# Last stage of a three-stage kernel: first blocks loaded during the d_ff stage into their own place, later loads ordered behind each unit's blocks, output product in order

## The chip, the cores and the metric

The kernel runs on one core of a Trainium2 chip. The metric is the device time of one execution in microseconds. TensorE (PE) does the matmuls and its weight loads (PEld), VectorE (DVE), ScalarE (ACT) and GpSimd (POOL) the elementwise work; loads and stores are issued from the queue of SyncE (SP), a few from POOL's.

## The reference

Three stages follow each other on 4608 tokens (8 batches of 576). Attention over a memory of 32 slots for each head gives x with 512 features; a layer with d_ff = 2048 and the activation h - tanh(h) gives x again; the last stage is a maximum over three projections and an output product:

```python
h = x @ w_in                       # 512 -> 2048
g = h - np.tanh(h)
x = g @ w_out                      # 2048 -> 512
h = np.maximum(np.maximum(x @ w1, x @ w2), x @ w3)   # 512 -> 768 each
return h @ w_out                   # 768 -> 512
```

## The kernel before

Everything is float32. A product that must keep its precision is made of three matmuls on operands split in a high part (rounded to float32r) and a low part (the rest): high x high, high x low, low x high. Splitting an operand costs a ScalarE copy (the high part) and a subtraction on VectorE or POOL (the low part).

The attention and d_ff stages run together up to about 821 us. `steps` lists the d_ff work: a tile of tokens and one of 16 chunks of 128 features; `emit_h` makes h, `emit_g` the activation, `emit_x` adds the chunk's contribution to four PSUM banks. At a tile's last chunk, VectorE adds the banks to `xo` and SP stores it in `xd[1]` (L531). Smaller work of other stages is dealt out in `slot()` as background; there `Paced` (L48) orders an instruction of VectorE, ScalarE or PE behind that engine's `mark`, the last instruction of the main work, without a semaphore.

The last stage works on six groups of 768 tokens. Each group has nine units (three column blocks `jp` by three projections `w`). A unit multiplies a block `sw` of weights with the group's x in the seven-product scheme of Strassen and Winograd: operands B11, T3, T1, B21, T2, B22, T4 (L633), seven products of six matmuls each with 384 columns, 42 in all, in four of six rotating PSUM banks. Between them ScalarE copies (p1, p5, u2), and VectorE and POOL add into `c` and take the running maximum in `m`. After the third projection of a column block, `m` is split into `mh` (L788 to L794), the upper half `q` 0 and 1 and one quarter on POOL, one quarter on VectorE. After nine units `outs` makes the output product: for each of six blocks of 128 tokens, 18 matmuls of 512 columns (six rows `j` of the weights `wz`), with banks b0 and b1 in turn, a copy into `ob`, and four stores.

The weights `sw` were laid out in DRAM as nine blocks of 1792 KB, and each unit loads its own again: four buffers sw0 to sw3, and `load_sw(n + 4)` at the end of unit n (L784), so that a load waits for the unit that used its buffer. `xprep` (L649) and `split` (L636) prepare a group's operands: the first group's during d_ff (`first_x`, a hook sixteen steps before the end of d_ff, L682; T4's split after it, L734), a later group's inside `outs` from `xr`, four parts of 384 KB loaded at the group's unit 0 (L839).

All memory of the last stage besides B11 to B22 (mv0 to mv5) comes from the pool `l`, which lies on the memory of attention and d_ff; a tile waits for the last reader of what lay there. The first four blocks are loaded after d_ff's instructions, three of them from POOL's queue (L733), the fourth and the six parts of `wz` from SP (L736 to L739). A program orders each engine's instructions ahead of time by when it expects them to be ready; on the chip each engine and each queue goes through its list in order. SP's transfers use eight semaphores in turn, so that a transfer's issue also waits for the eighth before it to land.

Of the kernel before, what the change touches and what calls it, by code (L numbers as in the profile page):

```python
# [7 lines left out]
F32 = mybir.dt.float32  # L8
F32R = mybir.dt.float32r
# [13 lines left out]
def kernel(  # L23
# [24 lines left out]
    class Paced:  # L48
# [4 lines left out]
        def __getattr__(self, name):  # L53
            op = getattr(self.engine, name)

            def call(*a, **kw):
                i = op(*a, **kw)  # L57
                if self.mark is not None and background[0]:
                    tc.add_manual_dep(i.ins, self.mark.name, mybir.DependencyInfo(mybir.DependencyClass.NoSync, mybir.DependencyReason.DATA), reason="pace")
                return i  # L60

            return call

    background = [False]
    V, S, T = (Paced(e) for e in (nc.vector, nc.scalar, nc.tensor))
    G, DMA = nc.gpsimd, nc.sync
    B, H, NS, D = q.shape
    M = phi.shape[3]
    P = 128
# [39 lines left out]
    def f(x):  # L109
        return x.bitcast(F32)  # L110
# [523 lines left out]
    mv_p, mv = [], {}  # L634

    def split(i, y, eng):  # L636
        t = get("mv6") if i == T4 else mv_p[0].tile([P, 2, 2, NQ], F32R, tag=f"mv{i}", bufs=1, name=f"mv{i}")
        S.copy(t[:, 0], y)
        yield
        if eng is G:  # L640
            for c in range(2):
                G.tensor_sub(t[:, 1, c], y[:, c], f(t[:, 0, c]))  # L642
                yield
        else:
            eng.tensor_sub(t[:, 1], y, f(t[:, 0]))
            yield
        mv[i] = t

    def xprep(x):  # L649
        b11, b12, b21, b22 = x  # L650
        yield from split(B11, b11, V)
        V.tensor_sub(b11, b12, b11)
        yield
        V.tensor_sub(b12, b22, b12)
        yield
        yield from split(T3, b12, G)
        yield from split(T1, b11, V)
        yield from split(B21, b21, G)
        V.tensor_sub(b11, b22, b11)
        yield  # L660
        yield from split(T2, b11, V)
        yield from split(B22, b22, G)
        V.tensor_sub(b21, b21, b11)
        yield

    def x_load(x, g):
        for y, kc, h in zip(x, (0, 0, 2, 2), (0, 1, 0, 1)):
            DMA.dma_start(out=y, in_=xd[1][:, kc:kc + 2, g * NG + h * NQ:g * NG + (h + 1) * NQ])

    def first_x():  # L670
        while bg.q:
            bg.step(10 ** 9)
        prep_s.close()
        pre_p = pool("pre", stack=last, side="right")
        mv_p.append(pre_p)
        x = [(pre_p if t == "xe" else cv_p).tile([P, 1024], F32, tag=t, bufs=n, name="xq")[:, :2 * NQ].rearrange("p (k c) -> p k c", k=2)
             for t, n in (("raw", 2), ("raw", 2), ("xe", 1), ("cs", 1))]
        x_load(x, 0)
        first_x.x = x
        bg.add("x", xprep(x), start[2, 0] - 12)  # L680
# [1 line left out]
    hooks[start[2, 0] - 16] = [first_x]  # L682
    run(start[1, 0], start[2, 0])
    wo1_p.__exit__(None, None, None)
    main.close()


    last2 = ExitStack()
    l_p = pool("l", stack=last2)
    ps_b = pool("ps_b", PSUM, last2)  # L690

    fresh = {}

    def lay(tag, shape, dt=F32, p=l_p):
# [7 lines left out]
    lay("sw0", [P, 2, 14, P], F32R)  # L702
    lay("mv6", [P, 2, 2, NQ], F32R)
    for i in range(3):
        lay(f"mh{i}", [P, 2, 2, NG], F32R)
    for n in ("p1", "p5", "u2"):
        for i in range(2):
            lay(f"{n}{i}", [P, NQ])
    for i in range(2):
        lay(f"ob{i}", [P, DM])  # L710
    lay("c", [P, 4, NQ])
    lay("gap", [P, 512])
    for i in (1, 2):
        lay(f"sw{i}", [P, 2, 14, P], F32R)
    for i in range(2):
        lay(f"m{i}", [P, 4, NQ])
    lay("wz", [P, J, 2, DM], F32R)
    lay("xr", [P, 4, 2, NQ])
    lay("sw3", [P, 2, 14, P], F32R)
    for i in range(8):  # L720
        lay(f"b{i}", [P, 512], F32, ps_b)

    sw_t = {}
    NU = 9 * GR

    def load_sw(n, dma=DMA):
        if n < NU:
            t = sw_t[n] = get(f"sw{n % 4}")
            dma.dma_start(out=f(t), in_=sw_d[n % 9])

    bg.need("x")
    for n in range(3):
        load_sw(n, G)  # L733
    for _ in split(T4, first_x.x[2], V):  # L734
        pass
    load_sw(3)  # L736
    wz = get("wz")
    for j in range(J):
        DMA.dma_start(out=f(wz[:, j]), in_=wz_d[j])  # L739

    free = [6, 7, 4, 5, 2, 3]
    acc, mh_t = [None], {}
# [1 line left out]
    def unit(n):  # L744
        jp, w = divmod(n % 9, 3)
        sw = sw_t.pop(n)
        ids = [free.pop(0) for _ in range(4)]
        A, Bk, Ck, Dk = (get(f"b{i}")[:, :NQ] for i in ids)
        i = n % 2

        def prod(o, s, x, first, final):
            for kc in range(2):
                st = sw[:, :, 2 * s + kc]
                x0, x1 = mv[x][:, 0, kc], mv[x][:, 1, kc]
                for k, (lt, rt) in enumerate(((st[:, 0], x0), (st[:, 0], x1), (st[:, 1], x0))):
                    T.matmul(o, lt, rt, start=first and kc == 0 and k == 0, stop=final and kc == 1 and k == 2, skip_group_check=True)

        if w == 0:
            acc[0] = get(f"m{jp % 2}")
        m = acc[0]  # L760

        c = m if w == 0 else get("c")

        def upd(q):
            if w:
                V.tensor_max(m[:, q:q + 2], c[:, q:q + 2], m[:, q:q + 2])

# [12 lines left out]
        prod(Ck, 6, B22, False, True)  # L780
        V.tensor_add(c[:, 1], Ck, u2)
        upd(0)
        prod(Bk, 2, T4, False, True)
        load_sw(n + 4)  # L784
        V.tensor_add(c[:, 2], Bk, u2)
        upd(2)
        free.extend(ids[k] for k in (3, 0, 2, 1))
        if w == 2:  # L788
            mh = mh_t[jp] = get(f"mh{jp}")
            for q, nq, e in ((0, 2, G), (3, 1, G), (2, 1, V)):  # L790
                h, t = divmod(q, 2)
                y, o = m[:, q:q + nq].rearrange("p a c -> p (a c)"), slice(t * NQ, (t + nq) * NQ)
                S.copy(mh[:, 0, h, o], y)
                e.tensor_sub(mh[:, 1, h, o], y, f(mh[:, 0, h, o]))  # L794

    def outs(g):
        ps = {}

        def part(u, js):
            if u not in ps:  # L800
                ps[u] = get(f"b{u % 2}")
            o = slice(u * P, (u + 1) * P)
            for j in js:
                mh = mh_t[j // 2][:, :, j % 2, o]
                mm3(ps[u], (mh[:, 0], mh[:, 1]), (wz[:, j, 0], wz[:, j, 1]), j == 0, j == J - 1)

        def done(u):
            ob = get(f"ob{u % 2}")
            (S.copy if u % 2 else V.tensor_copy)(ob, ps[u])
            for r in range(0, P, 32):  # L810
                b, j = divmod((g * NG + u * P + r) // 32, TJ)
                dst = out[b * NS:(b + 1) * NS, :].rearrange("(p j) e -> j p e", j=TJ)
                DMA.dma_start(out=dst[j], in_=ob[r:r + 32, :])

        prep = iter(())
        if g + 1 < GR:
            x = [xr[:, k] for k in range(4)]
            prep = chain(xprep(x), split(T4, x[2], V))
        for u in range(6):
            if u == 0:  # L820
                part(0, range(4))
                part(1, range(4))
                part(0, range(4, J))
            elif u == 1:
                part(1, range(4, J))
            else:
                part(u, range(J))
            done(u)
            for _ in range(6):
                next(prep, None)  # L830
# [42 lines left out]
```

## Time and profile before

| | us |
|---|---|
| median of 3 runs | 1394.51 (1391.09 to 1396.32) |
| the profiled execution | 1389.84 |
| its span, first to last instruction | 1388.1 |
| TensorE busy | 1289.5 (93%) |
| VectorE busy | 741.0 (53%) |
| POOL busy | 586.6 (42%) |
| ScalarE busy | 507.2 (37%) |

The profiled execution's time is its span and 1.7 us around it. Busy times are sums over the whole program; what a stage is bound by is read from the timeline, the windows and the waits of that stage. A matmul's record is longer than the time until the next one starts, because matmuls overlap: the pace is read from a run of many.

### The profile page before, as it was taken

The numbers are of one execution on the slowest core, as the hardware profiler recorded it, in microseconds if no ns is written. First come the engines' busy times: TensorE is split into PE (matmuls) and PEld (weight loads), VectorE is DVE, ScalarE is ACT, GpSimd is POOL, SyncE is SP. The second block draws the span as 40 slices with busy tenths as digits, with TensorE's granted clock in tenths as the row PEclk, the third lists the DMA queues.
The fourth block names the chain that finished last, engine by engine and source line by source line (L and its number), as shares of the span: only waits on it lengthen the run. The fifth ranks groups of instructions, "written<-read, shape, count | busy, mean of one in ns | idle before, by whom it ended". The sixth has DMA issues, their size and how long they took to land.

```text
span 1388.1 us, 22726 instructions
## 1 busy us (share of the span) xinstructions
PE 1289.5 (93%) x8996; PEld 1156.9 (83%) x8996; DVE 741.0 (53%) x1147; ACT 507.2 (37%) x993; POOL 586.6 (42%) x505
## 2 busy tenths in 40 slices
PE   3568888999999999999999989999999999999998
PEld 1446776887887798898889989989999899899996
DVE  4758646676445655765643333635734646357342
ACT  2425334454343554555544322322312223123121
POOL 4446334563323546675764332422512424235121
PEclk9979999999999999999999999999999999999999
DMA  8774747767524536666573159556656656565531
GB/s 222 175 205 150 177 146 203 179 210 187 137 102 171 176 117 233 228 210 253 206 252 117 50 217 411 213 197 237 233 168 250 235 175 218 192 247 190 166 134 46
DMA packets 179690, 264.94 MB, mean 191 GB/s; under 512 B 85760, under 2 KB 151552, under 8 KB 170496
## 3 DMA queue, kind: packets, MB, share of 16 engines
q1 hardware_dynamic: 178384, 256.80, 56.7%
q0 software_dynamic: 1200, 6.69, 1.4%
q8 instruction: 71, 1.16, 0.4%
q14 instruction: 35, 0.29, 0.1%
HBM read 199.49 MB, written 63.96 MB: 190 GB/s over the span
## 4 chain that ended last, share of the span: by engine, by line
PE 71%; DMA 10%; DVE 7%; POOL 6%; SPq 2%; ACT 2%; issue 2%; ACTq 0%; DVEq 0%; POOLq 0%
PE b L57 32%; PE ps_x L57 23%; PE ps_h L57 12%; DMA sw<-sw_d 3%; POOL mv L642 2%; PE ps_kv L57 2%; DVE cvb L57 2%; PE ps_w L57 2%; DMA wz<-wz_d 1%; SPq L198 1%; DMA raw<-in_moe_w_in_dram 1%; DMA kv<-in_v_dram 1%; POOL mh L794 1%; DVE s L57 1%; DVE st L57 1%
## 5 line engine op out<-in xcount | busy, mean ns | idle before, releaser
L57 PE MATMUL ps_x<-gh,wo 128*128 128x320 f32 (+2 forms) x2400 | 451.7, 335 | 14.9 <-DVE xo L57 10.4
L57 PEld LDWEIGHTS ps_x<-gh,wo 128*128 128x128 f32 x2400 | 379.6, 190 | 64.2 <-issue 22.9
L57 PE MATMUL b<-mv,sw 128*128 128x384 f32 x2268 | 410.3, 340 | 5.0 <-DMA sw<-sw_d 5.0
L57 PEld LDWEIGHTS b<-mv,sw 128*128 128x128 f32 x2268 | 403.7, 189 | 9.1 <-DMA sw<-sw_d 4.0
L496 POOL TENSOR_TENSOR gh<-th,gh 128x320 fp32r<-128x320 f32 (+2 forms) x200 | 210.4, 1054 | 241.2 <-ACT gh L57 232.4
L57 PE MATMUL ps_h<-at,vw 128*128 128x256 f32 (+2 forms) x1536 | 251.1, 304 | 29.2 <-ACT at L57 14.3
L57 PEld LDWEIGHTS ps_h<-at,vw 128*128 128x128 f32 x1536 | 225.2, 194 | 55.4 <-ACT at L57 16.1
L57 DVE TENSOR_TENSOR th<-ps_h,th 128x320 f32<-128x320 f32 (+2 forms) x200 | 106.7, 537 | 184.1 <-ACT th L57 182.5
L57 ACT ACTIVATE th<-ps_h 128x320 f32<-128x320 f32 (+2 forms) x200 | 94.9, 478 | 179.0 <-PE ps_h L57 173.1
L57 PE MATMUL b<-wz,mh 128*128 128x512 f32 x648 | 157.5, 393 | 2.9 <-POOL mh L794 2.3
L779 POOL TENSOR_TENSOR c<-c,u 128x384 f32<-128x384 f32 x36 | 40.1, 1113 | 276.0 <-ACT u L57 276.0
L57 PEld LDWEIGHTS b<-wz,mh 128*128 128x128 f32 x648 | 120.3, 188 | 29.6 <-POOL mh L794 4.3
L57 ACT CAST gh<-th 128x320 fp32r<-128x320 f32 (+2 forms) x200 | 99.7, 499 | 98.1 <-DVE th L57 84.8
L57 ACT COPY p<-b 128x384 f32<-128x384 f32 x108 | 51.8, 479 | 165.6 <-PE b L57 165.6
L794 POOL TENSOR_TENSOR mh<-m,mh 128x768 fp32r<-128x768 f32 (+1 forms) x36 | 67.8, 1903 | 50.8 <-ACT mh L57 50.8
L57 DVE TENSOR_TENSOR c<-b,u 128x384 f32<-128x384 f32 x72 | 39.7, 552 | 87.8 <-PE b L57 87.8
L57 DVE TENSOR_SCALAR cvb<-cvb 128x512 f32<-128x512 f32 x112 | 66.3, 592 | 32.6 <-ACT cvb L57 30.6
L57 DVE TENSOR_TENSOR m<-c,m 128x768 f32<-128x768 f32 x72 | 73.7, 1024 | 4.1
L57 DVE TENSOR_TENSOR vw<-ps_w,vw 128x512 fp32r<-128x512 f32 x64 | 41.4, 682 | 35.5 <-ACT vw L57 35.5
L57 DVE TENSOR_TENSOR c<-b,p 128x384 f32<-128x384 f32 x72 | 37.6, 554 | 42.1 <-ACT p L57 40.5
L642 POOL TENSOR_TENSOR mv<-xr,mv 128x384 fp32r<-128x384 f32 x30 | 45.0, 1524 | 28.7 <-ACT mv L57 28.7
L57 DVE COPY ob<-b 128x512 f32<-128x512 f32 x18 | 12.4, 689 | 81.3 <-PE b L57 81.3
(82 smaller groups left out, 1069.3 us busy)
## 6 DMA issues: line engine op xcount, KB each, us to landing
sw<-sw_d SPq DMA_DIRECT2D x51, 1792.0 KB, 7.4
sw_d<-so SPq DMA_DIRECT2D x9, 1792.0 KB, 6.2
raw<-in_moe_w_out_dram SPq DMA_DIRECT2D x22, 512.0 KB, 4.1
at_d<-at SPq DMA_DIRECT2D x16, 576.0 KB, 3.8
at<-at_d SPq DMA_DIRECT2D x8, 1152.0 KB, 6.2
raw<-in_moe_w_dram SPq DMA_DIRECT2D x18, 512.0 KB, 4.9
out_dram<-ob SPq DMA_DIRECT2D x144, 64.0 KB, 1.7
xd<-xo SPq DMA_DIRECT2D x14, 640.0 KB, 4.7
```

The source lines that it names most:

```text
L57: i = op(*a, **kw)
L198: q_dma.dma_start(out=t[64 * e + 32 * h:64 * e + 32 * h + 32, r], in_=src[e, h, r])
L496: G.tensor_sub(gh[:, 1], th, f(gh[:, 0]))
L642: G.tensor_sub(t[:, 1, c], y[:, c], f(t[:, 0, c]))
L779: G.tensor_add(c[:, 3], c[:, 3], u2)
L794: e.tensor_sub(mh[:, 1, h, o], y, f(mh[:, 0, h, o]))
```

## The change

The first block (sw0) gets a place in the pool `pre` beside mv0 to mv3, and `first_x` loads it on SP in front of the first group's x. x itself lies in an `at` buffer and in `cs`. A new pool `r`, opened after the last d_ff step on the place of d_ff's second-half output weights, holds mv4 to mv6, `xr`, `c` and the two `ob`; the splits of T2, B22 and T4 (`xrest`) come there, after the last d_ff step. Blocks 1 and 2 are still loaded from POOL's queue, block 3 from SP. The parts of `wz` are loaded one at a time at units 2 to 7 of the first group, and `xr` at unit 8 in the first group and unit 2 in the others, each ordered on SP behind the last block load. In `outs`, the matmuls are ordered behind the last unit's matmuls (`T.mark`), and the preparation of the next group behind the mh instructions of its engine (`S.mark`, `e.mark`), for which POOL is `Paced` too. The first half of `mh` (q 0 and 1) goes from POOL to VectorE. Its core:

```diff
-    V, S, T = (Paced(e) for e in (nc.vector, nc.scalar, nc.tensor))
-    G, DMA = nc.gpsimd, nc.sync
+    V, S, T, G = (Paced(e) for e in (nc.vector, nc.scalar, nc.tensor, nc.gpsimd))
+    DMA = nc.sync
...
-        yield from split(T2, b11, V)
-        yield from split(B22, b22, G)
         V.tensor_sub(b21, b21, b11)
         yield
...
+    def xrest(x):
+        return chain(split(T2, x[0], V), split(B22, x[3], G), split(T4, x[2], V))
...
+        sw_t[0] = pre_p.tile([P, 2, 14, P], F32R, tag="sw0", bufs=1, name="sw0")
+        DMA.dma_start(out=f(sw_t[0]), in_=sw_d[0])
+        t = at_p.tile([P, 3, 2, NQ], F32, tag="at", bufs=3, name="xq")
+        u = cv_p.tile([P, 1024], F32, tag="cs", bufs=1, name="xq")[:, :2 * NQ].rearrange("p (k c) -> p k c", k=2)
+        x = [t[:, 0], t[:, 1], u, t[:, 2]]
         x_load(x, 0)
...
+    r_p = pool("r", stack=last, side="right")
...
+    for _ in xrest(first_x.x):
+        pass
+    main.close()
...
-    for n in range(3):
+    for n in (1, 2):
         load_sw(n, G)
-    for _ in split(T4, first_x.x[2], V):
-        pass
     load_sw(3)
     wz = get("wz")
-    for j in range(J):
-        DMA.dma_start(out=f(wz[:, j]), in_=wz_d[j])
...
-                    T.matmul(o, lt, rt, start=first and kc == 0 and k == 0, stop=final and kc == 1 and k == 2, skip_group_check=True)
+                    T.mark = T.matmul(o, lt, rt, start=first and kc == 0 and k == 0, stop=final and kc == 1 and k == 2, skip_group_check=True).ins
...
-            for q, nq, e in ((0, 2, G), (3, 1, G), (2, 1, V)):
+            for q, nq, e in ((0, 2, V), (3, 1, G), (2, 1, V)):
...
-                S.copy(mh[:, 0, h, o], y)
-                e.tensor_sub(mh[:, 1, h, o], y, f(mh[:, 0, h, o]))
+                S.mark = S.copy(mh[:, 0, h, o], y).ins
+                e.mark = e.tensor_sub(mh[:, 1, h, o], y, f(mh[:, 0, h, o])).ins
...
         def part(u, js):
+            background[0] = True
...
+            background[0] = False
...
+            background[0] = True
             for _ in range(6):
                 next(prep, None)
+            background[0] = False
...
-            if n == 0 and g + 1 < GR:
+            late = []
+            if g == 0 and 2 <= n < 2 + J:
+                late.append(DMA.dma_start(out=f(wz[:, n - 2]), in_=wz_d[n - 2]))
+            if n == (2 if g else 8) and g + 1 < GR:
                 xr = get("xr")
-                x_load([xr[:, k] for k in range(4)], g + 1)
+                late += x_load([xr[:, k] for k in range(4)], g + 1)
+            for d in late:
+                behind(d.ins, load_sw.last)
```

`behind` is the ordering without a semaphore that `Paced` used before, as a function. `load_sw` now keeps its last load in `load_sw.last`.

## Rows read from the trace of the kernel before

**Rows 1.** The page, part 1: busy us (share of the span), instructions.
```profile
PE 1289.5 (93%) x8996; PEld 1156.9 (83%) x8996; DVE 741.0 (53%) x1147; ACT 507.2 (37%) x993; POOL 586.6 (42%) x505
```

**Rows 2.** Timeline of PE: start, length, tile, count, idle before and releaser.
```profile
814.08 6.76 PE L57 MATMUL ps_x<-gh,wo 128*128 128x320 f32 x45
824.56 30.44 PE L57 MATMUL b<-mv,sw 128*128 128x384 f32 x156 [3.72 <-DMA sw<-sw_d]
856.30 15.92 PE L57 MATMUL b<-mv,sw 128*128 128x384 f32 x89 [1.30 <-DMA sw<-sw_d]
```

**Rows 3.** Windows: length, each engine's busy time (count), granted clock, DMA share, GB/s.
```profile
730.00:760.00 30.00, 30.00 (x230) 26.99 (x229) 12.17 (x24) 13.44 (x29) 12.20 (x13) 1.00 0.37 127
...
820.80:824.50 3.70, 0.04 (x1) 0.00 (x0) 1.75 (x4) 0.00 (x0) 0.00 (x0) 0.88 0.98 415
824.50:832.00 7.50, 7.44 (x27) 7.44 (x28) 0.80 (x2) 0.96 (x2) 0.00 (x0) 0.60 1.02 417
...
840.00:848.00 8.00, 8.00 (x48) 8.00 (x47) 4.00 (x6) 1.44 (x3) 1.02 (x1) 1.00 1.03 402
...
883.30:907.30 24.00, 23.62 (x127) 22.23 (x126) 19.78 (x21) 10.16 (x17) 14.26 (x10) 1.00 0.62 229
```

**Rows 4.** Chain in order of time, 815 to 910: start, length, what.
```profile
823.97 19.39 DMA wz<-wz_d
...
843.43 12.73 DMA sw<-sw_d
```

**Rows 5.** Waits of PE, 860 us to the end: total, times, longest.
```profile
PE b L57 <- POOL mh L794: 2.3, 6, 0.4
```

**Rows 6.** Timeline, last group: two runs of matmuls without a break.
```profile
1339.72 15.70 PE L57 MATMUL b<-mv,sw 128*128 128x384 f32 x88
...
1366.61 16.66 PE L57 MATMUL b<-wz,mh 128*128 128x512 f32 x72 [0.56 <-DVE ob L57]
```

**Rows 7.** Timeline of SP near 735 us: the first load of x.
```profile
734.74 0.37 SPq L668 DMA_DIRECT2D xq<-xd  x1
```

**Rows 8.** Timeline around the end of d_ff: splits, block loads, last sums.
```profile
795.35 2.00 POOL L642 TENSOR_TENSOR mv<-xq,mv 128x384 fp32r<-128x384 f32 x2 [0.21 <-ACT mv L57]
...
804.57 3.29 POOL L642 TENSOR_TENSOR mv<-xq,mv 128x384 fp32r<-128x384 f32 x2 [1.80 <-ACT mv L57]
...
815.70 0.83 ACT L57 CAST mv<-xq 128x768 fp32r<-128x768 f32 x1
...
816.70 1.70 POOL L729 DMA_DIRECT2D sw<-sw_d  x3
820.00 1.68 DVE L57 TENSOR_TENSOR xo<-ps_x,xo 128x320 f32<-128x320 f32 x4 [4.70 <-PE ps_x L57]
821.60 0.95 DVE L57 TENSOR_TENSOR mv<-xq,mv 128x768 fp32r<-128x768 f32 x1
```

**Rows 9.** DMA by window (816.6 on, 822.9 to 829, 860 to 930): KB, us to landing; share.
```profile
sw<-sw_d POOLq DMA_DIRECT2D x1, 1792.0 KB, 7.8
...
q0 software_dynamic: 201, 2.45, 95.1%
...
sw<-sw_d SPq DMA_DIRECT2D x7, 1792.0 KB, 7.7
```

**Rows 10.** Timeline, last group: what mh needs after its last product.
```profile
1360.58 0.55 DVE L57 TENSOR_TENSOR c<-b,u 128x384 f32<-128x384 f32 x1
...
1361.23 0.96 DVE L57 TENSOR_TENSOR m<-c,m 128x768 f32<-128x768 f32 x1
...
1362.22 0.93 ACT L57 CAST mh<-m 128x384 fp32r<-128x384 f32 x2 [0.69 <-DVE m L57]
1363.18 1.12 DVE L57 TENSOR_TENSOR mh<-m,mh 128x384 fp32r<-128x384 f32 x1 [0.99 <-ACT mh L57]
```

**Rows 11.** Timeline: preparation for the second group, first cast and last subtraction.
```profile
888.16 0.84 ACT L57 CAST mv<-xr 128x768 fp32r<-128x768 f32 x1
...
905.43 2.59 DVE L57 TENSOR_TENSOR mv<-xr,mv 128x768 fp32r<-128x768 f32 x1
```

More of the change, by code (lines that the diff above doesn't have):

```diff
@@ L58, in call, with behind @@
                 if self.mark is not None and background[0]:
-                    tc.add_manual_dep(i.ins, self.mark.name, mybir.DependencyInfo(mybir.DependencyClass.NoSync, mybir.DependencyReason.DATA), reason="pace")
+                    behind(i.ins, self.mark)
                 return i
             return call
+    def behind(ins, mark):
+        tc.add_manual_dep(ins, mark.name, mybir.DependencyInfo(mybir.DependencyClass.NoSync, mybir.DependencyReason.DATA), reason="pace")
     background = [False]
-    V, S, T = (Paced(e) for e in (nc.vector, nc.scalar, nc.tensor))
-    G, DMA = nc.gpsimd, nc.sync
+    V, S, T, G = (Paced(e) for e in (nc.vector, nc.scalar, nc.tensor, nc.gpsimd))
+    DMA = nc.sync
     B, H, NS, D = q.shape
@@ L636, in split @@
     def split(i, y, eng):
-        t = get("mv6") if i == T4 else mv_p[0].tile([P, 2, 2, NQ], F32R, tag=f"mv{i}", bufs=1, name=f"mv{i}")
+        t = get(f"mv{i}") if i > B21 else mv_p[0].tile([P, 2, 2, NQ], F32R, tag=f"mv{i}", bufs=1, name=f"mv{i}")
         S.copy(t[:, 0], y)
@@ L666, in x_load @@
     def x_load(x, g):
-        for y, kc, h in zip(x, (0, 0, 2, 2), (0, 1, 0, 1)):
-            DMA.dma_start(out=y, in_=xd[1][:, kc:kc + 2, g * NG + h * NQ:g * NG + (h + 1) * NQ])
+        return [DMA.dma_start(out=y, in_=xd[1][:, kc:kc + 2, g * NG + h * NQ:g * NG + (h + 1) * NQ])
+                for y, kc, h in zip(x, (0, 0, 2, 2), (0, 1, 0, 1))]
+    def xrest(x):
+        return chain(split(T2, x[0], V), split(B22, x[3], G), split(T4, x[2], V))
+    sw_t = {}
     def first_x():
@@ L675, in first_x @@
         mv_p.append(pre_p)
-        x = [(pre_p if t == "xe" else cv_p).tile([P, 1024], F32, tag=t, bufs=n, name="xq")[:, :2 * NQ].rearrange("p (k c) -> p k c", k=2)
-             for t, n in (("raw", 2), ("raw", 2), ("xe", 1), ("cs", 1))]
+        sw_t[0] = pre_p.tile([P, 2, 14, P], F32R, tag="sw0", bufs=1, name="sw0")
[3 more added lines that the diff above has]
+        x = [t[:, 0], t[:, 1], u, t[:, 2]]
         x_load(x, 0)
@@ L684, with lay @@
     wo1_p.__exit__(None, None, None)
[L685 to L690, printed above, removed]
+    bg.need("x")
+    r_p = pool("r", stack=last, side="right")
     fresh = {}
-    def lay(tag, shape, dt=F32, p=l_p):
+    def lay(tag, shape, dt, p):
         fresh[tag] = [shape, dt, p, p.tile(shape, dt, tag=tag, bufs=1, name=tag)]
@@ L700, in get @@
         return s[2].tile(s[0], s[1], tag=tag, bufs=1, name=tag) if t is None else t
-    lay("sw0", [P, 2, 14, P], F32R)
-    lay("mv6", [P, 2, 2, NQ], F32R)
+    for i in (T2, B22, T4):
+        lay(f"mv{i}", [P, 2, 2, NQ], F32R, r_p)
+    lay("xr", [P, 4, 2, NQ], F32, r_p)
+    lay("c", [P, 4, NQ], F32, r_p)
+    for i in range(2):
+        lay(f"ob{i}", [P, DM], F32, r_p)
+    for _ in xrest(first_x.x):
+        pass
+    main.close()
+    last2 = ExitStack()
+    l_p = pool("l", stack=last2)
+    ps_b = pool("ps_b", PSUM, last2)
+    fresh["sw0"] = [[P, 2, 14, P], F32R, mv_p[0], None]
+    lay("sw3", [P, 2, 14, P], F32R, l_p)
+    lay("m0", [P, 4, NQ], F32, l_p)
     for i in range(3):
-        lay(f"mh{i}", [P, 2, 2, NG], F32R)
+        lay(f"mh{i}", [P, 2, 2, NG], F32R, l_p)
     for n in ("p1", "p5", "u2"):
         for i in range(2):
[L708 to L712, printed above, removed]
-    for i in (1, 2):
[L714 to L719, printed above, removed]
+            lay(f"{n}{i}", [P, NQ], F32, l_p)
+    lay("m1", [P, 4, NQ], F32, l_p)
+    for i in (1, 2):
+        lay(f"sw{i}", [P, 2, 14, P], F32R, l_p)
+    lay("wz", [P, J, 2, DM], F32R, l_p)
     for i in range(8):
         lay(f"b{i}", [P, 512], F32, ps_b)
-    sw_t = {}
     NU = 9 * GR
@@ L728, in load_sw @@
             t = sw_t[n] = get(f"sw{n % 4}")
-            dma.dma_start(out=f(t), in_=sw_d[n % 9])
-    bg.need("x")
-    for n in range(3):
+            load_sw.last = dma.dma_start(out=f(t), in_=sw_d[n % 9]).ins
+    for n in (1, 2):
         load_sw(n, G)
-    for _ in split(T4, first_x.x[2], V):
-        pass
     load_sw(3)
     wz = get("wz")
-    for j in range(J):
-        DMA.dma_start(out=f(wz[:, j]), in_=wz_d[j])
     free = [6, 7, 4, 5, 2, 3]
@@ L817, in outs @@
             x = [xr[:, k] for k in range(4)]
-            prep = chain(xprep(x), split(T4, x[2], V))
+            prep = chain(xprep(x), xrest(x))
         for u in range(6):
```

## The prediction

> **What bounds the kernel now.** I read the busy table first: TensorE (PE) works 1289.5 of 1388.1 us, 93% [rows 1]. So a change pays only where PE stands still or runs at half clock in the stretch that it touches, which is the last stage, from about 820 us. There the PE timeline shows what to price [rows 2]: d_ff's last matmul ends at 814.08 + 6.76 = 820.84, the first matmul of the last stage starts at 824.56 after a wait for the load of sw0, and the stream breaks again before 856.30, for the load of a later block. The windows show the third loss [rows 3]: from 824.5 to 832 the granted share is 0.60 and only 27 matmuls run in 7.5 us, where a full-clock window holds 48 in 8 us. The clock fell while PE stood (0.88 in the gap itself). The chain names who was late [rows 4]: SyncE's queue (SP) waited for the second projection's weights wz until 843.36, then issued the block for unit 4, and that landed 12.73 us later. In the rest of the stage PE's own waits are 2.3 us in six places for mh [rows 5] and 0.6 us in one place for ob, before the last run of the output product [rows 6].
>
> **The yardstick.** A steady run of 88 unit matmuls takes 15.70 us with the last one's 0.34, so (15.70 - 0.34)/87 = 0.1766 us each; a unit of 42 is 7.4 us. For the output product, (16.66 - 0.39)/71 = 0.229 us each; a group's 108 are 24.7 us [rows 6].
>
> **Opening: what is removed.** 156 matmuls lie between 820.84 and 856.30 [rows 2]. At full pace they need 156 x 0.1766 = 27.5 us, and they took 35.5. The loss is 7.9 us: 3.7 of gap, about 2.7 of half clock, about 1.5 before 856.30. All of it hangs on loads. The change loads sw0 some 80 us earlier into a place of its own. SP issues it in front of the first group's x loads, the first of which goes out at 734.74 [rows 7]; from 730 to 760 us the DMA share is 0.37 with PE at 30.00 of 30.00 us [rows 3], so 1.84 MB (some 4.4 us at the 415 GB/s of the full stretch) hides; that cover gone, it would cost those 4.4 us at most, and the x loads behind it on SP are wanted by the splits of d_ff's last 30 us, such as those in [rows 8]. The six wz loads leave the opening, each going behind a later unit's block on SP, so nothing is queued there ahead of unit 4's block. A unit then draws 1.84 + 0.52 MB in 7.4 us, 319 GB/s, below the 402 to 417 that the full windows move. The wz loads end near 888 us; the product first needs j = 4 and 5 after 24 matmuls, at 893. I cost these at nothing.
>
> **Opening: what is added.** The splits of T2, B22 and T4 move to the end of d_ff: 3 ScalarE casts, 2 VectorE and 2 GpSimd (POOL) subtractions. The last split of before shows the place: its cast starts at 815.70, its subtraction at 821.60 behind the four xo sums [rows 8]. With 0.83 us a cast, the casts end near 816.5, 817.4 and 818.2; the VectorE subtractions end at 822.6 and 823.6; unit 0 wants T2 at 820.84 + 4 x 1.06 = 825.1, T4 at 827.2. So they hide, with 2 us to spare. What stands behind them on POOL matters more: the loads of sw1 and sw2. Before, POOL issued three blocks at 816.70 [rows 8], the first landing after 7.8 us [rows 9]. Now B22's two subtractions come first, 1.0 us each beside an idle VectorE, 1.65 beside a busy one (2.00 and 3.29 for two [rows 8]). From 817.4 on, that is an issue at 819.5 (818.8 to 820.9), and sw1 lands at 827.3 (826.6 to 828.7). Unit 0 ends at 820.84 + 7.4 = 828.2. I take 0.3 us of stall, bounds 0 and 0.5 with the casts in this place. sw2 waits for the readers of the x tile beneath it, until 822.6, and lands before 833 against a need at 835.7; sw3 comes 4.4 us later. SP's store of xo can't push sw1 back much: with both queues full POOL's held 95.1% of the DMA engines' time [rows 9].
>
> What the trace doesn't show is POOL writing these descriptors beside a busy VectorE: at 816.7 to 818.4 VectorE was idle, at 819.5 to 820.7 the xo sums begin [rows 8]. The nearest row is the stretch of POOL's subtraction from 1.0 to 1.65 us, and I keep 0.3 for the stall. The Trainium skill, SBUF — State Buffer, section "SBUF: two separate sides", speaks against this place: a load issued from GpSimd has its descriptors written by GpSimd, which certain VectorE operations on SBUF lock out, so that the load stands still meanwhile. By that rule the load waits for VectorE; its result is the third rival.
>
> **Group boundaries.** Before, the output product's matmuls were mixed into unit 8 and the next group's preparation ran ahead of mh on POOL; PE then waited for mh. Now the 24 matmuls of j 0 to 3 stand together behind unit 8: 24 x 0.229 = 5.5 us of cover. Beneath them mh's last part needs, after unit 8's last product: VectorE's sum and maximum (0.55 and 0.96), ScalarE's two small casts (0.93), VectorE's last subtraction (1.12) [rows 10] and, at worst between them, the subtraction of the first quarter pair that comes over from POOL (0.95, as the split of the same shape in [rows 8]): 4.5 us. That fits with 1.0 us to spare. So PE's waits on mh go, 2.3 us, and the 0.6 for ob, since six matmuls (1.4 us) lie between a bank's end and its reuse and a copy takes 0.7: 2.9 us. Restarting the weight loads after a wait may add up to 0.13 at each of seven places; ends 0 and 3.8, I take 2.9. The moved subtraction costs VectorE those 0.95 us a group; VectorE is busy 19.8 of 24 us at the boundary [rows 3], but there it is mostly preparation, which now starts later. That delay is the cover to watch: the preparation ran from 888.16 to 908.0, 19.9 us [rows 11]. Starting 4 us after the units' end it is through 24 us after it, where the product lasts 24.7 and the last operand is wanted 6.4 later: 7 us to spare. Nothing is late next there.
>
> In groups 1 to 4 the x load moves from unit 0 to unit 2 and still has 45 us. In group 0 it moves to the end of unit 8, behind the block for unit 12, whose issue waits for unit 8's last matmul. With unit 8 ending at 820.84 + 0.3 + 378 x 0.1766 = 887.9, that block lands 7.7 us later [rows 9], at 895.6, and the four x parts at 0.95 us each until 899.4. The preparation then ends near 916 to 919, where T4 is wanted at 887.9 + 24.7 + 6.4 = 919.0. I cost it at nothing, bounds 0 and 7.6 (second rival).
>
> **Sum**, against the profiled execution of 1389.84 us: 7.9 - 0.3 + 2.9 = 10.5, so 1379.3. The median of the runs shown is 4.7 above that execution, so I give 1394.5 - 10.5 = 1384.0. Its own bounds, 11.7 and 6.5 of gain with the ends above, give 1382.8 to 1388.0 at the median, and the runs of before spread from 3.4 below it to 1.8 above.
>
> **Rivals.**
> 1. The wait moves from sw0 to sw1. If the splits can only start when d_ff's last matmul has ended (their new place lies on weights of d_ff), the casts run from 820.9, POOL's subtractions end near 825.9, sw1 lands at 833.7 and PE stands 5.5 us, with half clock after it as before (2.7). The opening gains 7.9 - 8.2 = -0.3, the whole 2.6: 1391.9. For it: new tiles on d_ff's memory. Against: the cast at 815.70 ran before d_ff's end on just such memory [rows 8]. Chance 0.13.
> 2. Group 0's x load comes late and an engine in order pays: if VectorE holds operations on x ahead of the first output copy, that copy (due 894.7) waits until 899.0 to 901.0, and the third block of the product, due 896.0, stands 2.9 to 4.9 us, with 2.7 more if the clock falls. At 5 us the gain is 5.5: 1389.0. For it: the load is issued when it is nearly due, where before it came 50 us early. Against: engines' orders follow expected readiness. Chance 0.14.
> 3. Descriptors late: if sw1's are written only when VectorE rests at 823.6, it lands at 830.9 and PE stands 2.7 us, short of the 2.8 after which the clock fell in the gap of before. Gain 8.1: 1386.4. The rule of the skill's SBUF page would do this; the rows so far bear out only POOL's slowing. Chance 0.08.
> 4. Slower: the preparation, held behind mh, comes onto the path at each of five boundaries. It decides at 4 + L > 31.1, so L above 27 us where before shows 19.9. At L = 31 PE stands 3.9 us and loses 2.7 to the clock, 6.6 x 5 = 33, less 10.5: 1417. For it: in-order placing takes away the freedom to fill. Against: the 7 us of room. Chance 0.10.
>
> **How the numbers follow.** Forecast 0.55, rivals 0.13, 0.14, 0.08, 0.10. About 0.5%, 7.0 us, is what a measurement of this kernel can tell from no change. Faster by more: the forecast but for its low end (0.53), rival 3 (0.07), a light case of rival 2 (0.02): 0.62. Within: the rest of forecast and rivals 2 and 3, and rival 1: 0.28. Slower: 0.10. The range reaches from 1379.5 (gain 11.7 at the lowest run of before) to 1392.5 (rival 1), leaving out rival 4 and a tail.
>
> **What would show it.** Right: the first unit matmul within 0.2 us of d_ff's last, no half-clock row near 823, no wait before unit 4, a wait for sw under 1 us before unit 1; PE's waits for mh gone; the product's matmuls after each unit 8 in one block. Wrong: a gap of several us before unit 1 or in group 0's product, waits for mv at the boundaries, or a break elsewhere in the opening that the wait for sw0 hid so far.

## The result, and the profile after

| | us |
|---|---|
| median before, 6 runs beside the change | 1392.33 |
| median of the change, 6 runs | 1380.08 (1377.07 to 1383.0) |
| ratio | 0.9907, 95% interval 0.9889 to 0.9925 |
| profiled execution: time, span | 1377.07, 1375.3 |

The forecast was 10.5 us; the medians differ by 12.3, and the ratio stands for 12.9 (10.4 to 15.5). The chance given for faster by over 0.5% was borne out, and the median lies near the range's lower end, 1379.5, with the profiled execution below it. More was won than was reckoned. The forecast of 1384.0 us for the median stood on the 3 runs of before that were shown, 1394.5; the six beside the change give 1392.33, so 2.2 of the 3.9 us by which it was too high lie in that base.

The page of the changed kernel, its span and busy times. TensorE does the same matmuls, 8996, in 1288.1 us, as in [rows 1]; only the span is shorter.

```profile
span 1375.3 us, 22722 instructions
...
PE 1288.1 (94%) x8996; PEld 1160.7 (84%) x8996; DVE 742.8 (54%) x1165; ACT 507.6 (37%) x993; POOL 542.1 (39%) x486
```

The timeline of PE where [rows 2] have the gap: start, length, tile, count.

```profile
816.27 6.32 PE L57 MATMUL ps_x<-gh,wo 128*128 128x320 f32 x42
822.43 9.74 PE L57 MATMUL b<-mv,sw 128*128 128x384 f32 x55
```

d_ff's last matmul ends at 816.27 + 6.32 = 822.59, and the first unit's has begun by then. The windows of the changed kernel answer [rows 3]: length, busy time (count) by engine, granted clock, DMA share, GB/s.

```profile
690.00:720.00 30.00, 30.00 (x171) 26.53 (x170) 13.69 (x24) 14.44 (x27) 18.48 (x15) 1.00 0.83 307
822.60:830.00 7.40, 7.40 (x44) 7.40 (x44) 4.29 (x9) 1.44 (x3) 1.57 (x2) 1.00 1.00 351
830.00:856.00 26.00, 26.00 (x150) 25.99 (x149) 11.87 (x19) 6.95 (x14) 4.42 (x4) 1.00 0.95 379
```

The clock is 1.00 where it was 0.60, and 44 matmuls run in 7.4 us. The DMA engines are as full as before, but with blocks that PE does not yet stand for. Of the chain of waits these five pieces are all that the last stage has, besides slivers of up to 0.04 us and the last copy to ob (start, length, what):

```profile
822.59 74.36 PE b L57 x413
...
896.98 0.70 DVE ob L57
...
897.72 455.44 PE b L57 x2429
...
1353.19 0.70 DVE ob L57
...
1353.93 16.65 PE b L57 x72
```

From 822.59 to the end PE stands only for two copies to ob (DVE ob). The waits for loads of [rows 4] and those for mh of [rows 5] are gone.

To compare kernels I use one measure below, the **stretch**: from the start of d_ff's last matmul to the start of the last matmul of all. It leaves out the stages before, whose end moves from execution to execution: it fell at 820.84 in the execution of before and from 822.4 to 830.3 in the thirteen profiles of the change and the experiments. The spells at half clock before it all lie in the first 452 us and differ in number and length; the last 1500 matmuls up to that end take 228.5 to 228.9 us in all fourteen profiles, so the early load of sw0 costs them 0.4 us at most. That also is why the profiled execution of before lay 4.7 us under its median. The stretch was 562.3 us before and 547.9 in the change: 14.4 us won, of which the later end of d_ff hides 1.75 between these two executions. A **loss**, below, is what the time from the start of one matmul to the start of the next has above its steady pace.

### The profile page after: what moved, and what is told of

Same layout as the page of the kernel before. It is cut to its first block, busy times and chain, and to the rows that moved or that the text cites. A ratio compares the mean times of both kernels' runs of the same rounds, so it can differ in the third digit from the quotient of the medians.

```text
span 1375.3 us, 22722 instructions
## 1 busy us (share of the span) xinstructions
PE 1288.1 (94%) x8996; PEld 1160.7 (84%) x8996; DVE 742.8 (54%) x1165; ACT 507.6 (37%) x993; POOL 542.1 (39%) x486
## 4 chain that ended last, share of the span: by engine, by line
PE 82%; DVE 7%; DMA 5%; ACT 2%; POOL 2%; SPq 1%; issue 1%; ACTq 0%; POOLq 0%; DVEq 0%
PE b L57 40%; PE ps_x L57 24%; PE ps_h L57 13%; PE ps_kv L57 2%; PE ps_w L57 2%; DMA kv<-in_v_dram 1%; DVE s L57 1%; DVE cvb L57 1%; DVE st L57 1%; DMA raw<-in_moe_w_in_dram 1%; POOL s L57 1%; DMA raw<-in_moe_w_out_dram 1%; DMA xd<-xo 1%; DVE qT L57 1%; DVE aT L57 1%
## 5 line engine op out<-in xcount | busy, mean ns | idle before, releaser
L57 PEld LDWEIGHTS ps_x<-gh,wo 128*128 128x128 f32 x2400 | 384.7, 192 | 61.5 <-issue 23.9
L57 PE MATMUL b<-mv,sw 128*128 128x384 f32 x2268 | 401.3, 338 | 0.0
L57 PEld LDWEIGHTS b<-mv,sw 128*128 128x128 f32 x2268 | 399.2, 188 | 1.1
L57 PE MATMUL ps_h<-at,vw 128*128 128x256 f32 (+2 forms) x1536 | 252.7, 306 | 27.5 <-ACT at L57 15.5
L57 PE MATMUL b<-wz,mh 128*128 128x512 f32 x648 | 150.4, 390 | 1.1 <-DVE ob L57 1.1
L57 POOL TENSOR_TENSOR c<-c,u 128x384 f32<-128x384 f32 x36 | 36.6, 1015 | 226.0 <-ACT u L57 226.0
L57 DVE TENSOR_TENSOR m<-c,m 128x768 f32<-128x768 f32 x72 | 69.0, 958 | 5.0
L57 POOL TENSOR_TENSOR mv<-xr,mv 128x384 fp32r<-128x384 f32 x30 | 48.9, 1664 | 12.2 <-ACT mv L57 12.2
L57 POOL TENSOR_TENSOR m<-m,u 128x384 f32<-128x384 f32 x18 | 21.2, 1175 | 82.0 <-ACT u L57 80.7
L57 ACT CAST mh<-m 128x384 fp32r<-128x384 f32 (+1 forms) x54 | 31.8, 620 | 57.1 <-DVE m L57 57.1
```

## The experiments

| kernel | stretch us | against the change | ratio to before, 95% interval |
|---|---|---|---|
| before | 562.3 | +14.4 | |
| the change | 547.9 | | 0.9907 (0.9889 to 0.9925) |
| the change once more | 548.2 | +0.3 | 0.9895 (0.988 to 0.991) |
| opening alone | 554.4 | +6.5 | 0.9941 (0.9925 to 0.9957) |
| ordering alone | 558.4 | +10.5 | 0.9958 (0.9943 to 0.9974) |
| sw0's load moved in the code | 548.4 | +0.5 | 0.9888 (0.9862 to 0.9913) |
| sw0 behind d_ff | 553.6 | +5.7 | |
| wz at once | 551.2 | +3.3 | |
| product's matmuls not ordered | 555.5 | +7.6 | |
| preparation not ordered | 549.5 | +1.6 | |
| mh's first half on POOL | 548.1 | +0.2 | |
| neither preparation ordered nor mh on VectorE | 554.7 | +6.8 | |
| banks in order | 546.7 | -1.2 | 0.9893 (0.9870 to 0.9916) |
| banks in order, B22 on VectorE | 554.6 | +6.7 | 0.9926 (0.9904 to 0.9948) |

Each stretch is that of one execution, and below the row of before, one without a ratio is the only execution of its kernel. Two executions of the same program, the change and the change once more, differ by 0.3 us in the stretch, so a few tenths are not read; where PE stands for a load, what the half clock behind it costs differs too, from nothing to 2.8 us (last section).

> The change once more, beside the two that follow on one chip. Stretch from d_ff's last matmul to the last one 547.9 us within 0.3, while the end of d_ff, where the program is the same as before but for the last steps, falls anywhere between 820 and 828 us with the half-clock stretches of the first 450 us.

**The two halves, each alone.** The opening alone:

```diff
-                    T.mark = T.matmul(o, lt, rt, ...).ins
+                    T.matmul(o, lt, rt, ...)
-            for q, nq, e in ((0, 2, V), (3, 1, G), (2, 1, V)):
+            for q, nq, e in ((0, 2, G), (3, 1, G), (2, 1, V)):
-                S.mark = S.copy(mh[:, 0, h, o], y).ins
+                S.copy(mh[:, 0, h, o], y)
```

and without `e.mark`, without the pacing in `part` and around the preparation, and with POOL not `Paced`.

> The change without its ordering of the output product: no marks on the unit matmuls and on mh, no pacing in the output product, the first half of mh on POOL again; the early sw0, the places, the late wz and xr stay. Theory A (the terms of the prediction: opening 7.6, boundaries 2.9): 7.6 us faster than before, PE's waits on mh still about 2.3 us in six places. Theory B (the boundaries are worth about twice what their wait rows say, since every matmul that waits restarts its weight load): the stretch from d_ff's last matmul to the end, 562.3 us before and 547.9 after, becomes 554.1, 8.2 below before. Rival C (the late xr and wz pay only in an ordered product): over 2 us of new waits in the first group, gain under 6.

The ordering alone is the same edit the other way round, on the kernel before.

> The kernel before with the ordering alone: matmuls of the output product behind the last unit's, preparation behind mh, the first half of mh on VectorE; the opening as before. Theory A: 2.9 us faster than before, the opening's gap, half clock and wait for unit 4 unchanged. Theory B: 4.3 to 6.2 us faster, the stretch from d_ff's last matmul to the end 556.1 to 558. Rival C (the ordering uncovers waits that the early xr and the mixed product hid): not faster.

The opening alone won 7.9 us, where theory A said 7.6 and theory B 8.2. The ordering on top of it won 6.5, more than twice A's 2.9. The ordering without the opening won 4.0 in its profiled execution, and PE's timeline there says why it was so little:

```profile
826.64 29.33 PE L57 MATMUL b<-mv,sw 128*128 128x384 f32 x156 [3.54 <-DMA sw<-sw_d]
858.59 6.63 PE L57 MATMUL b<-mv,sw 128*128 128x384 f32 x28 [2.62 <-DMA sw<-sw_d]
```

The gap before unit 0 is there as in [rows 2], and the wait before unit 4 is 2.62 us where it was 1.30, again for a block load, with half clock after it. The ordering has no part in that: the block lands 35.4 us after d_ff's end here and 35.3 before, but PE comes to it 1.3 us earlier, since ten matmuls ran at half clock behind the first gap instead of seventeen, and the longer stand then brought the half clock a second time. In groups 1 to 4, where no load is waited for, the ordering saves the same 0.95 us a group: 92.3 us from one group's matmuls to the next before, 91.3 in this kernel; the losses at all boundaries fell from 6.0 us to 0.8. The ratio over ten executions stands for 5.9 us (3.6 to 8.0), that of the opening alone for 8.2 (6.0 to 10.5). Their sum, 14.1, can't be told from the 12.9 and 14.6 of the two measurements of the change, so nothing shows that the halves need each other. B holds for the size; rival C's longer wait came, but not from the ordering.

**What in the opening does it.** First sw0's load, moved to POOL's queue after the last step of d_ff in the code, its place left as it is:

```diff
-        DMA.dma_start(out=f(sw_t[0]), in_=sw_d[0])
...
+    G.dma_start(out=f(sw_t[0]), in_=sw_d[0])
     for n in (1, 2):
         load_sw(n, G)
```

> The change, but sw0 is loaded into its own place only after the last d_ff step, from POOL's queue ahead of sw1 and sw2, as before. Both theories: the gap before the first unit matmul comes back, with the half clock behind it; since POOL issues sw0 only behind B22's split, near 821.5, it lands near 829.3 and the gap is 6.5 to 7 us rather than 3.7; the half clock costs 2.5; in all 9 to 9.5 us slower than the change. Rival C (the wz loads behind the units were the larger part): under 4 us slower.

That did not do what it was meant to: the load still went out at 699.40 us, since its place was free. In the change SP issues it at 697.27. It says that the early load comes from the place and not from the line or the queue. The next kernel orders it behind POOL's last subtraction of d_ff:

```diff
-        G.tensor_sub(gh[:, 1], th, f(gh[:, 0]))
+        emit_g.last = G.tensor_sub(gh[:, 1], th, f(gh[:, 0])).ins
...
+    behind(G.dma_start(out=f(sw_t[0]), in_=sw_d[0]).ins, emit_g.last)
```

> The change, but sw0's load, from POOL's queue, is ordered behind POOL's last subtraction of d_ff; the place is its own. (In the run that only moved the load's line, it still went out at 699 us, since its place was free.) Theory: issued about 3.5 us before d_ff's last matmul ends, landing 7.8 us later: a gap of 4 us before the first unit matmul, half clock of 2.5 us behind it, and sw1 lands 4.4 us after sw0, before it is wanted. Stretch 554 to 555.5. Rival (the gap's price lies in wz alone): stretch under 551.

PE's timeline from the first unit on, and the windows of the gap and behind it:

```profile
826.19 33.98 PE L57 MATMUL b<-mv,sw 128*128 128x384 f32 x183 [3.82 <-DMA sw<-sw_d]
```

```profile
822.30:826.20 3.90, 0.08 (x2) 0.01 (x1) 2.64 (x5) 0.00 (x0) 0.53 (x1) 1.00 0.98 408
826.20:830.00 3.80, 3.80 (x13) 3.80 (x14) 0.00 (x0) 0.48 (x1) 0.00 (x0) 0.56 1.00 417
```

A gap of 3.8 us and a spell at 0.56 of the clock, 5.4 us more than the change once more: a little under the 6 expected. Behind the gap 10 matmuls ran at half clock here, 17 in the kernel before, which is 1.1 us of it. The rest of the opening is wz:

```diff
     wz = get("wz")
+    for j in range(J):
+        DMA.dma_start(out=f(wz[:, j]), in_=wz_d[j])
...
-            if g == 0 and 2 <= n < 2 + J:
-                late.append(DMA.dma_start(out=f(wz[:, n - 2]), in_=wz_d[n - 2]))
```

> The change, but the six wz loads go out together behind the load of sw3, as before. Measured by the stretch from d_ff's last matmul to the last one, 547.9 us in the change. Theory A (wz stood in front of unit 4's block on SP's queue: that wait of 1.45 us was its price): the wait before unit 4 comes back. With unit 0 starting 3.7 us earlier against the loads' queue than before and at full clock, unit 4 comes about 6 us earlier after its block's issue, so the wait grows to 4 to 7 us, with half clock behind it; stretch 553 to 557. Rival (the queue has room once sw0 is out of it): no wait over 0.5 us, stretch 548.

```profile
824.08 27.80 PE L57 MATMUL b<-mv,sw 128*128 128x384 f32 x156
854.55 5.68 PE L57 MATMUL b<-mv,sw 128*128 128x384 f32 x31 [2.67 <-DMA sw<-sw_d]
```

The wait before unit 4 is back, 2.67 us for a block load and the stretch 3.3 us longer: theory A's cause, at less than its price, since the wait was under the 4 us expected and the clock stayed full this time. The chain in this kernel shows two parts: SP issues the block only when the store of xo, the eighth transfer before it, has landed (837.31, or 13.1 us after d_ff's end, where the change issues it 7.3 us after), and behind the six wz loads it takes 17.06 us to land. In the kernel before, the second group's four x parts stood in front of that block as well:

```profile
835.25 7.20 SPq L668 DMA_DIRECT2D xr<-xd  x4
```

The change moves them to unit 8. No run moves them back, so what they added to the wait before unit 4 stays open; wz alone is enough for one.

**What in the ordering does it.** Each of its three parts was taken away by itself. The pacing of the product's matmuls:

```diff
         def part(u, js):
-            background[0] = True
```

> The change without the ordering of the output product's matmuls behind the last unit; the preparation stays behind mh, mh's first half on VectorE. Stretch 547.9 in the change, 554.4 with the whole ordering undone. Theory A (the waits at the boundary come from POOL doing the next group's preparation ahead of mh): the matmul order alone matters little, stretch 548 to 549.5. Rival B (a matmul of the product that was placed into unit 8 stands in front of the unit's own and waits for mh): stretch 552 to 554, breaks of 0.3 to 0.7 us in front of wz matmuls at each boundary.

It cost 7.6 us, more than the 6.5 that the ordering had won. The timeline of one boundary there:

```profile
986.32 2.69 PE L57 MATMUL b<-wz,mh 128*128 128x512 f32 x11
...
989.91 0.39 PE L57 MATMUL b<-wz,mh 128*128 128x512 f32 x1
...
991.20 1.09 PE L57 MATMUL b<-wz,mh 128*128 128x512 f32 x4
...
992.65 1.20 PE L57 MATMUL b<-wz,mh 128*128 128x512 f32 x4 [0.36 <-ACT mh L57]
...
994.18 2.12 PE L57 MATMUL b<-wz,mh 128*128 128x512 f32 x8 [0.34 <-DVE mh L57]
```

Of the 24 matmuls of cover, eight ran in the 40 us before these lines, eleven and one stand inside unit 8, and four are left behind it (991.20). Then the cover is used up: the first matmul that needs mh waits 0.36 us for ScalarE, the next 0.34 for VectorE. That is rival B's cause: the matmuls are spent inside the unit, though the wait comes behind the unit and not in it, and it cost more than B's 552 to 554. The pacing of the preparation:

```diff
-            background[0] = True
             for _ in range(6):
                 next(prep, None)
-            background[0] = False
```

> The change without the ordering of the preparation behind mh; the output product stays in order. Theory A: POOL's and VectorE's preparation runs ahead of mh again, mh comes late by 2 to 4 us, of which the 24 matmuls in front hide all but 0 to 2 us: stretch 549 to 556. Rival B: the 5.5 us of cover hide all of it, stretch 547.9 within 0.5.

1.6 us more: PE's weight loads wait 1.3 us in four places for an operand of the next group (mv), and mh is never late. So the number lies in theory A's range, but its cause is another, and rival B's 547.9 fell too. Columns: total, times, longest.

```profile
PEld b L57 <- DVE ob L57: 2.0, 2, 1.0
PEld b L57 <- POOL mv L57: 1.3, 4, 0.4
```

And mh's first half back on POOL:

```diff
-            for q, nq, e in ((0, 2, V), (3, 1, G), (2, 1, V)):
+            for q, nq, e in ((0, 2, G), (3, 1, G), (2, 1, V)):
```

> The change with mh's first half back on POOL (2.3 us there, 0.95 on VectorE). Theory (the ordering gives cover enough): POOL does 2.3 + 1.1 us after ScalarE's cast, 1.0 us later than VectorE's chain, within the cover of 5.5 us: stretch 547.9 within 0.5. Rival (the move to VectorE was what took the wait away): a wait for POOL's mh of 0.3 to 1 us at each of six boundaries, stretch 550 to 554.

0.2 us, nothing that can be read, as the theory said. So I thought that the order of the matmuls alone would carry the gain, and took the other two parts away together.

> The change with only the matmuls of the output product ordered: the preparation isn't held behind mh, and mh's first half is on POOL again. Theory (the order of the matmuls carries the gain at the boundaries, the other two give cover that is mostly not needed): stretch 549.5 to 551. Rival (without them POOL's mh is late by more than the 5.5 us of cover): stretch 552 to 556, with waits of PE for POOL's mh at each boundary.

My theory fell: 554.7 us, 0.8 of it lost to a wait for sw1 before unit 1 in this execution. The timeline of one boundary shows how:

```profile
1169.00 5.62 PE L57 MATMUL b<-wz,mh 128*128 128x512 f32 x24
...
1170.89 1.74 POOL L57 TENSOR_TENSOR c<-c,u 128x384 f32<-128x384 f32 x1
...
1172.58 3.42 POOL L57 TENSOR_TENSOR mv<-xr,mv 128x384 fp32r<-128x384 f32 x2
...
1175.96 3.83 POOL L57 TENSOR_TENSOR mh<-m,mh 128x768 fp32r<-128x768 f32 x2
...
1178.55 0.73 PE L57 MATMUL b<-wz,mh 128*128 128x512 f32 x2 [0.90 <-POOL mh L57]
```

The 24 matmuls stand behind the unit as they should. But POOL does two subtractions of the next group's preparation (1172.58, 3.42 us) between the sum for c (1170.89) and mh, and begins mh only at 1175.96; PE waits at 1178.55 although the cover was there. To keep mh in time, holding back the preparation, or moving mh's larger part off POOL, is enough by itself; with neither, 5.5 us of cover are too short.

**A step further.** The two waits for ob that were left come from the scheduler mixing the last matmuls of the first two banks. One more order:

```diff
-                mm3(ps[u], (mh[:, 0], mh[:, 1]), (wz[:, j, 0], wz[:, j, 1]), j == 0, j == J - 1)
+                last = mm3(ps[u], (mh[:, 0], mh[:, 1]), (wz[:, j, 0], wz[:, j, 1]), j == 0, j == J - 1)
             background[0] = False
+            T.mark = last
```

> The change with one ordering more: each part of the output product also behind the part before it, so that the two banks' last matmuls are no longer mixed (in the change, the first two banks end within one matmul of each other, and PE waits 0.72 us for a copy to ob in the first and in the last group). Theory: the 0.72 us and the restart of 0.11 go in both groups, 1.6 us faster than the change, stretch to the end 546.2. Rival: the strict order moves the wait elsewhere (the operands of the next group's first unit, or mh's last part) and the gain is nil.

Both waits went; what PE's weight loads still wait for in the whole last stage is one line:

```profile
PEld b L57 <- DMA sw<-sw_d: 0.6, 1, 0.6
```

The stretch is 1.2 us shorter, the expected 1.6 less a wait for sw1. Its ratio to before, 0.9893, can't be told from the change's. Then the first group's B22 on VectorE, so that POOL issues sw1 earlier:

```diff
-    for _ in xrest(first_x.x):
+    for _ in xrest(first_x.x, V):
```

with `split(B22, x[3], e)` in `xrest`.

> The change with the parts of the output product in order, as in the run with the banks in order, and the first group's B22 subtracted on VectorE, so that POOL issues sw1 right behind its last work of d_ff. Theory: sw1 is issued near 2.5 us earlier against d_ff's end, lands 2 us or more before unit 1, and the 0.1 to 0.6 us that PE lost before unit 1 in several runs go; stretch 546.1. Rival: VectorE's splits, behind the four xo sums, come too late for B22's product in unit 0 (wanted 5.3 us after its start): a break there of up to 1 us, stretch 547.

Neither case came: sw1 went out 3.7 us before d_ff's end and was in time, but sw2 wasn't. POOL's queue, PE, and the landing of that load (KB, us):

```profile
826.59 0.62 POOL L57 DMA_DIRECT2D sw<-sw_d  x1
833.17 0.57 POOL L57 DMA_DIRECT2D sw<-sw_d  x1 [5.96 <-DVE mv L57]
```

```profile
830.13 12.75 PE L57 MATMUL b<-mv,sw 128*128 128x384 f32 x72
848.60 11.56 PE L57 MATMUL b<-mv,sw 128*128 128x384 f32 x50 [5.72 <-DMA sw<-sw_d]
```

```profile
sw<-sw_d POOLq DMA_DIRECT2D x1, 1792.0 KB, 15.3
```

sw2 waits for VectorE's splits, which read the x beneath it, and goes out at 833.17, after SP's sw3 at 831.77; it took 15.3 us to land. PE stood 5.72 us and then ran at half clock. That is the size of my first rival (5.5 and 2.7), one block later and from another cause. The profile is of the slowest of four executions (1380.9 to 1391.51), but their median, 1385.44, against 1379.25 for the change once more beside it, says much the same.

## Why the prediction was right or wrong, step by step

Of the 14.4 us between the two profiled executions, counted from start to start of the matmuls, the opening is 8.2 (7.6 reckoned), the boundaries are 4.35 (2.9 reckoned), and 1.9 are a faster pace, which the prediction put at nothing.

**The opening, 7.6 us, held, in part by luck.** The opening alone gave 7.9. But that is 8.0 of waits and half clock gone and 1.2 of a faster pace, less 1.3 that were lost at the boundaries, where the losses grew from 6.0 to 7.3; the two terms that weren't reckoned nearly cancel. The parts came as reckoned: sw0 early is worth 5.4 to 5.7, wz behind the units 3.3. Together they exceed the whole, because the gap before unit 0 hides part of the wait before unit 4 (1.30 us with that gap, 2.67 without it). sw0's issue was read wrongly: it went out at 697.27, some 120 us earlier than before and not 80, and not beside the x loads (738.46). It did no harm: PE is busy 30.00 of 30.00 us while it lands, in the windows above.

**The split's move and sw1, 0.3 us of stall, held.** The end of d_ff in the changed kernel, all engines:

```profile
819.53 2.00 POOL L57 TENSOR_TENSOR mv<-xq,mv 128x384 fp32r<-128x384 f32 x2 [0.58 <-ACT mv L57]
821.48 0.62 POOL L57 DMA_DIRECT2D sw<-sw_d  x1
821.75 1.68 DVE L57 TENSOR_TENSOR xo<-ps_x,xo 128x320 f32<-128x320 f32 x4 [4.26 <-PE ps_x L57]
...
823.36 1.81 DVE L57 TENSOR_TENSOR mv<-xq,mv 128x768 fp32r<-128x768 f32 x2
...
824.07 0.67 SPq L739 DMA_DIRECT2D sw<-sw_d  x1
824.87 0.57 POOL L57 DMA_DIRECT2D sw<-sw_d  x1 [2.77 <-issue]
```

Everything is where the prediction put it, 1.75 us later with d_ff's end: B22's subtractions 1.0 us each, sw1's issue 1.1 us before that end, and sw2's at 824.87, while VectorE reads x, though the profile names no releaser for it. The landing of sw1's load:

```profile
sw<-sw_d POOLq DMA_DIRECT2D x1, 1792.0 KB, 7.8
```

7.8 us, and no wait in this execution; in the others with the early sw0 and this split, PE lost 0.1 to 0.8 us there. The margin is nil, as the bounds of 0 to 0.5 said, and slightly worse. **The third rival fell**: sw1 did not wait until VectorE rested. It took 7.8 us beside VectorE's sums and splits (821.75 to 825.17), as beside an idle VectorE [rows 9]; in the nine other executions with this issue it took 8.0 to 8.9, up to 1.1 us longer, and what that comes from isn't shown. The rule of the Trainium skill, SBUF — State Buffer, "SBUF: two separate sides", is not contradicted in general, since it speaks of certain operations, but a load that stands until VectorE rests is not seen at this place.

**The boundaries, 2.9 us, are the step that failed.** The mechanism was right, the term was mis-sized: the losses there fell by 4.35 us from the kernel before to the change, and the ordering was worth 6.5 on top of the opening, 5.6 of it at the boundaries. I counted PE's own waits. The weight loads wait first and longer. Their waits before, from 860 us to the end (total, times, longest), and those of the changed kernel:

```profile
PEld b L57 <- POOL mh L794: 4.3, 6, 0.9
PEld b L57 <- DVE mh L57: 2.0, 5, 0.4
PEld b L57 <- DVE ob L57: 1.0, 1, 1.0
```

```profile
PEld b L57 <- DVE ob L57: 2.0, 2, 1.0
```

7.3 us in twelve places, against the 2.9 in seven that I read in [rows 5] and [rows 6]. The first boundary's break before:

```profile
907.26 0.74 PE L57 MATMUL b<-wz,mh 128*128 128x512 f32 x2 [0.38 <-POOL mh L794]
```

From start to start of the matmuls, each boundary before lost 0.89 us: 0.53 at the one break that PE's waits show as 0.4, and 0.36 at three matmuls behind it that wait without PE standing, since their weights load late (0.34 us instead of 0.23). Five boundaries and 1.5 us in the last group make 6.0; the change keeps 1.65 of it, the two waits for ob. I had allowed 0.13 for a restart at each of seven places and then left it out. The loss is larger still in the opening alone, 7.3 us, with the product and the preparation as free as before and the x parts of the first group late; POOL's mh is waited for 5.4 us there, 4.3 before:

```profile
PEld b L57 <- POOL mh L799: 5.4, 6, 1.5
PEld b L57 <- DVE ob L57: 2.0, 2, 1.0
PEld b L57 <- DVE mh L57: 1.2, 3, 0.4
PEld b L57 <- DMA sw<-sw_d: 0.2, 1, 0.2
```

**The 0.6 us for ob did not go.** I argued that six matmuls lie between a bank's end and its reuse. The scheduler mixed the two banks' last twelve, so both end together: 0.70 us of copy in the chain above at 896.98 and 1353.19. With the banks in order both waits went.

**The cover for mh held, with the margin that was reckoned.** The first boundary of the changed kernel:

```profile
888.80 8.37 PE L57 MATMUL b<-wz,mh 128*128 128x512 f32 x36
...
889.50 0.55 DVE L57 TENSOR_TENSOR c<-b,u 128x384 f32<-128x384 f32 x1
...
890.15 0.96 DVE L57 TENSOR_TENSOR m<-c,m 128x768 f32<-128x768 f32 x1
891.03 2.24 DVE L57 TENSOR_TENSOR mh<-m,mh 128x768 fp32r<-128x768 f32 x2
891.14 0.93 ACT L57 CAST mh<-m 128x384 fp32r<-128x384 f32 x2 [0.69 <-DVE m L57]
891.74 1.12 POOL L57 TENSOR_TENSOR mh<-m,mh 128x384 fp32r<-128x384 f32 x1 [3.15 <-ACT mh L57]
```

From VectorE's sum at 889.50 to the end of its last subtraction at 893.27 are 3.8 us, less than the 4.5 reckoned, but the sum begins 0.7 us after the first product matmul. The 25th product matmul begins at 894.28, so 1.0 us is left, as reckoned; that it is the same to the tenth is luck.

**The second rival fell**: the x parts of the first group landed at 899 to 902 us, as reckoned (899.4 and 1.75 later), but VectorE's copy to ob stood in front of the operations that waited for them. **The fourth**, the preparation on the path, fell too: no wait for mv in the change, 0.3 us a boundary where the preparation was free. The preparation, reckoned at 19.9 us as before, took 13.2 to 13.7 once it stood behind mh. It had less time than reckoned, though: only the first 36 product matmuls after each unit 8 stand in one block (72 behind the first and all 108 behind the last group), and the next group's unit begins among the rest, 8.2 us after the product's first matmul in groups 1 to 4. So the sign "in one block" did not come as it was written. **The first**, a stand of 5.5 us for the next block, came only for sw2 and where I caused it.

**Smaller slips.** The low end of the gain, 6.5 us, doesn't follow from the ends given, which make 7.9 - 0.5 + 0 = 7.4. The gain by the ratio, 12.9, lies above the high end of 11.7, which had no room for the faster pace. And the 2.8 us of the third rival, the stand after which the clock fell before, is no bound: 2.62 us in the ordering alone were enough.

**The rest.** 1.9 us of the 14.4 lie in no wait. A unit matmul starts 176.4 to 176.6 ns after the one before in the kernel before and in the ordering alone, and 175.9 in every kernel with the change's places and loads, 1.2 us over 2268. That goes with the opening half, and neither the late sw0 nor wz at once brings the slower pace back. In the change it differs by buffer, 174.8 ns on sw0 and 176.7 on sw2, where before all four have 176.4 or 176.5; that speaks for the places, which were not tried by themselves. The product's matmuls are 0.6 us faster in all: 228.5 ns before, in the opening alone and (228.6) without their order, 227.5 in the change and in the ordering alone. That goes with the order of the product's matmuls; why is not shown.

## What to carry to other kernels

Price a stall on TensorE from start to start of its matmuls and from the waits of its weight loads; the matmul's own waits showed under half of it here. Independent matmuls that stand ready as cover for a late operand are worth something only if the scheduler can't spend them earlier: order them, and hold back what shares an engine with the late operand. A load that opens a stage is best given a place that nothing else holds; here it then went out early by itself, from either queue that was tried.

## What the runs showed of the hardware

What a stand of PE costs beside itself differed between like stands. At half clock a unit matmul starts 320 ns after the one before, at full clock 176. In the kernel before (gap of 3.72 us) and with the banks in order and B22 on VectorE (5.72), 16 or 17 matmuls ran so, which lost 2.6 to 2.8 us; with sw0 behind d_ff (3.82) and twice in the ordering alone (3.54 and 2.62), 8 to 10, which lost 1.5 to 1.6. After 2.67 us with wz at once the clock did not fall at all. So a stand of some 3 us was followed by a loss of 0 to 2.8 us here, and what decides between them isn't shown.

Of two block loads on different queues, POOL's landed first when it was issued 0.8 us behind SP's (824.87 and 824.07 above, landed at 834.75 and 839.43), and last when 1.4 us behind (833.17 and 831.77, landed at 848.47 and 844.18). The prediction had reckoned with POOL's queue winning.
